# A reordered first stage and a spread first sweep in a fused attention, gated MLP and token/channel mixer kernel

## The chip, the core and the metric

One Trainium2 chip, one core. The metric is the device time of one execution in microseconds. Before the change it is 1242.53 us, the median of 3 runs (1241.91 to 1242.74). The execution that was profiled took 1244.85 us, of which the traced span is 1242.3 us.

## The reference, cut

Three layers follow each other, for 8 batches of 576 tokens (S) and 512 features:

```python
# 1: attention in chunks of 64 tokens, 8 heads of 64
scores = scale * q_c @ k_c.T; attn = exp(scores - max); attn /= sum + 1e-9
x = attn @ v_c                                   # (8, 576, 512)
# 2: gated MLP with a product over tokens
h = relu(x @ w_in); u, v = h[..., :512], h[..., 512:]
v_n = (v - mean(v)) / sqrt(var(v) + 1e-6)
x = (u * (w_spatial @ v_n + b_spatial)) @ w_out
# 3: mixer
u = x + (relu(x.T @ w_tok1) @ w_tok2).T
out = u + relu(u @ w_ch1) @ w_ch2                # d_tok 256, d_ch 1536
```

All inputs reach the kernel as 32-bit or 64-bit floats; `w_in`, `w_out` and the weights of the mixer come in 64 bits and are converted on the chip.

## The kernel before, in words

Each large product runs in a split form: an operand is kept as a rounded high part and a low part, and three matmuls (high by high, high by low, low by high: `PASSES`) take the place of one. So nearly every operand costs one cast on ACT (the high part) and one subtraction on DVE that waits for that cast (the low part).

The work has four parts. **The first stage** (about the first 120 us) does the attention and the gated MLP of batch 0, begins the attention of batch 1, and converts the weights on the way. **The steady stages** do the same for batches 1 to 6, with the attention of the next batch in between, and store each batch's result in device memory (`x2d`). **The last stage** does the gated MLP of batch 7 and in its gaps begins the mixer for batch 0. **The sweeps** do the mixer's channel half: eight sweeps of 21 groups for the first product (`ch1`), then eight of 7 for the second (`ch2`). The channel products use seven block products in place of eight, so they work on seven combinations of the operand (`comb_u`, 0 to 6) and of the weights (`Comb`, sets 0 to 3).

The order of the first, steady and last stages is written out by hand in three strings (`FIRST`, `STEADY`, `LAST`, from line 24). `play` (line 1169) reads them word by word; each word is one step, and each engine executes its instructions in the order in which they were so recorded. The words of the first stage that matter here, where a number behind the word is a unit, a column block or a piece:

- `x`, `S`, `s`, `e`, `n`, `z`, `T`, `t`, `P`, `p`, `q` are one head pair's attention: transposing q and k on DVE (line 377), scores on PE (391), the maximum and the subtraction on DVE (410, 411), exp on ACT (417), the sum on DVE (421), scaling on POOL (427), transposing on PE (435), its copy on ACT (443), the product with v on PE (459), and the result's high part on ACT (478) and low part on DVE (480). With an `a` ahead they belong to batch 0, without it to batch 1 here.
- `wl`, `wa`, `wm`, `we`, `wi`, `wk` (or `wj`) convert piece 0 to 11 of `w_in` and `w_out`: load (130), two scalings on ACT (144, 145), two bit operations on DVE (153, 155), an addition on POOL (163), the high part on ACT (185) and the low part on POOL or DVE (188). Pieces 0 to 3 are the rows of the half of `w_in` that makes v; pieces 4 to 7 are the columns of the half that makes u, one for each of `U0` to `U3`; pieces 8 to 11 are `w_out`.
- `gl`, `gt`, `gh` load `w_spatial`, transpose one column block on PE (246) and split it (83, 84; the last block 256, 257 and 262 to 264).
- `Y`, `V`, `R`, `r`, `F`, `G`, `rs`, `rq`, `N`, `i`, `Q` make v and normalize it: products on PE (536, 565), relu on ACT (583), statistics on DVE (588, 589), the fold of the last 64 tokens (574, 575, 579), the root (593 to 598), the normalization on DVE (602), and its split (608, 617). `U`, `E` make u (625, relu 635). `W`, `M`, `H`, `J` make the product over tokens and the gate (648, 658, 661, 664), `A`, `B`, `O`, `D` the output product (674, 681).

Two PSUM buffers tie steps together. `turn_ws` (the word `gt`) and `pv` (the word `P`) write the same buffer, tag `p`, of which there is one; so a `P` waits until the `gh` ahead of it has read the transposed block, and the reverse. `U` and `W` rotate through two buffers, so `U2` waits for the relu of `U0`.

In the mixer, the token half of batch b+1 runs inside sweep b, one step after each group (`tok_steps`, line 936): `b_nat` (860) transposes 128 token rows on DVE (866), rounds them on ACT (868) and makes the low part on DVE (870 or 873) in one go; `b_tok1` (879) multiplies them on PE (887, 891, 893); `b_tok2` (919) makes the second token product (926), which DVE adds (931). Ahead of sweep 1 the steps for batch 1 have already begun at the end of `LAST` (`st`, `st2`), and all seven `comb_u` of batch 0 are made there (`cu0` to `cu6`; casts 967, low parts 968, differences 974). In sweep 1 the weights of the groups 7 to 20 are still to be made: the dictionary `fill` lists which step of `comb_steps` (casts 821, low parts 825, sums on POOL 809 to 813) follows which group. `ch1_out` (1033) reads the results (1039 to 1051, 1030).

Of the kernel before, what the change touches and what calls it, by code (L numbers as in the profile page):

```python
# [23 lines left out]
FIRST = """  # L24
al0 wl0 al1 wl1 Z9 ax0 ay0 wa0 aS0 as0 ax1 al2 av0 wl2 wm0 ae0 ay1 an0 we0 az0 aS1 as1 wa1 aT0 wi0 wm1
at0 ax2 al3 av1 wl3 we1 wk0 ae1 ay2 an1 az1 aP0 aS2 ap0 as2 wi1 aq0 aT1 wa2 ae2 at1 ax3 av2 wm2 ay3 an2
az2 aP1 av3 aS3 as3 ap1 ae3 aq1 wj1 ax4 ay4 aT2 we2 wa3 wi2 at2 an3 wm3 az3 gl0 gl1 gl2 wl4 wl5 aP2 aS4
as4 ap2 wk2 we3 aq2 Y0 ae4 aT3 at3 wi3 an4 wk3 az4 Y1 aP3 L0 ap3 aq3 wa4 aT4 at4 Y2 aP4 wm4 ap4 aq4 Y3
x0 we4 wl6 wa5 L1 gt0 wi4 R0 R1 gh0 wm5 r0 S0 V2 s0 wk4 R3 we5 gt1 wi5 F r1 e0 R2 r3 wa6 G r2 gh1 wk5
U0 wl7 n0 x1 R4 z0 wm6 gt2 r4 we6 rs rq gh2 wi6 S1 U1 E0 wk6 s1 N0 T0 gt3 wa7 i0 Q0 t0 e1 gh3 N1 U2  # L30
wm7 n1 N2 we7 gt4 i1 wi7 E1 z1 Q1 gh4 wk7 i2 N3 N4 L2 wl8 U3 i4 Q2 x2 P0 p0 L3 S2 i3 E2 Q3 T1 q0 Q4
W0 t1 E3 s2 wl9 wa8 wm8 wa9 W1 we8 x3 e2 M0 M1 wi8
wm9 S3 W2 n2 wl10 we9 H0 wa10 W3 M2 s3 H2 wi9 J0 wl11 M3 z2 P1 S4 wk8 H1 J1 wj9 p1 q1 J2 H3
e3 wm10 T2 J3 A0 s4 n3 we10 A1 wa11 t2 L4 z3 wi10 B0 wm11 D0 e4 B1 P2 p2 D1 we11 T3 wj10 O2 n4
q2 t3 x4 z4 L5 P3 T4 wi11 p3 q3 D2 wk11 t4 O3 P4 D3 p4 q4
"""
# [19 lines left out]
def attention_gmlp_mixer(  # L56
# [794 lines left out]
    def b_load(b, m):  # L851
# [7 lines left out]
                in_=x2d[b][:, 32 * e:32 * e + 32].rearrange("(t j) i -> j t i", j=32))  # L859
        raws[b, m] = raw  # L860

    def b_nat(b, m):
# [5 lines left out]
        nc.scalar.copy(out=xn[:, 0], in_=nat)  # L868
        if m < 4:
            nc.vector.tensor_tensor(  # L870
                out=xn[:, 1], in0=nat, in1=f32(xn[:, 0]), op=ALU.subtract)
        else:
            nc.vector.tensor_tensor(
                out=xn[64:128, 0], in0=nat[64:128], in1=f32(xn[64:128, 0]), op=ALU.subtract)
# [4 lines left out]
    def b_tok1(b, m, xn):
        if m == 0:  # L880
            tok[b] = [PB["ps_t"].tile([128, 512], F32, tag="t", name="ps_h1") for _ in range(2)]
        ps = tok[b]
        for kk in range(2):
            ksl = slice(128 * kk, 128 * kk + 128)
            if m < 4:
                for n, (p, r) in enumerate(PASSES):
                    nc.tensor.matmul(  # L887
                        ps[kk], lhsT=PB["w1"][r][:, m, ksl], rhs=xn[:, p],
                        start=m == 0 and n == 0, stop=False)
            else:  # L890
                nc.tensor.matmul(
                    ps[kk], lhsT=PB["w1r"][0][:, ksl], rhs=xn[:, 0], start=False, stop=False)
# [387 lines left out]
    put_in(0, 6, c1[2][1].load)  # L1280
    put_in(0, 7, s1[2][0][0])
    put_in(0, 8, *s1[2][0][1:3], s1[2][1][0])
    put_in(0, 9, s1[2][0][3], s1[2][1][1])
    put_in(0, 10, s1[2][0][4], s1[2][1][2])
    put_in(0, 11, s1[2][1][3])
    put_in(0, 12, s1[2][1][4])
# [105 lines left out]
```

## Time and profile before

| | |
|---|---|
| median of 3 runs | 1242.53 us |
| the profiled execution: own time, span | 1244.85 us, 1242.3 us |
| PE busy (matmuls) | 1192.9 us, 96% of the span |
| DVE, ACT, POOL busy | 879.5 us (71%), 501.0 us (40%), 161.7 us (13%) |
| mean granted TensorE clock | 0.984 |
| DMA | 196.00 MB, mean 158 GB/s |

The rows of the profile give a start in us from the span's start, a duration in us, the engine, the line, the operation, the tiles written and read and their shapes; in square brackets stands the idle time of that engine just before, and what ended it. "PE" rows are matmuls; a run of equal ones is one row. In the tables by stretch each engine has its busy time and the number of its instructions, and then come the granted clock, the DMA share and the rate. The profiled execution's own time is 2.55 us longer than its span (1244.85 - 1242.3): this lies around the traced instructions.

### The profile page before, as it was taken

How to read it: one execution, taken by the hardware profiler on the slowest of the kernel's cores; microseconds unless marked ns; L12 is line 12 of the kernel's file. 1: busy time of each engine (PE TensorE's matmuls, PEld its weight loads, DVE VectorE, ACT ScalarE, POOL GpSimd, SP SyncE). 2: the span in 40 equal slices, each digit the busy share in tenths (PEclk: the TensorE clock that was granted, in tenths of full speed). 3: DMA queues.
4: the chain of work that ended last, by engine and by line, in shares of the span. 5: the costliest groups of instructions: out<-in, count | busy, mean ns of one | idle time of the engine just before them, and what ended most of it. 6: DMA issues, size and time to landing. Idle time of an engine off the chain costs nothing. (4 is left out here: it accounts for less than half of the span.)

```text
span 1242.3 us, 25079 instructions
## 1 busy us (share of the span) xinstructions
PE 1192.9 (96%) x10042; PEld 1127.6 (91%) x10042; DVE 879.5 (71%) x1365; ACT 501.0 (40%) x797; POOL 161.7 (13%) x156
## 2 busy tenths in 40 slices
...
GB/s 228 150 77 127 96 104 134 100 172 107 200 85 206 89 213 38 56 158 203 140 142 170 170 189 172 163 187 166 134 303 190 195 217 199 183 188 189 214 213 45
DMA packets 405704, 196.00 MB, mean 158 GB/s; under 512 B 348434, under 2 KB 368338, under 8 KB 405588
## 3 DMA queue, kind: packets, MB, share of 16 engines
...
q8 instruction: 79, 1.29, 0.5%
...
HBM read 123.16 MB, written 71.17 MB: 156 GB/s over the span
## 5 line engine op out<-in xcount | busy, mean ns | idle before, releaser
L1010 PE MATMUL ps_c<-ub,wt 128*128 128x288 f32 x2016 | 288.9, 298 | 6.6 <-ACT s L1042 2.5
L1010 PEld LDWEIGHTS ps_c<-ub,wt 128*128 128x128 f32 x2016 | 278.2, 190 | 12.9 <-ACT s L1042 3.8
L1010 PE MATMUL ps_c<-hb,wt 128*128 128x288 f32 x2016 | 268.9, 295 | 1.6 <-DVE hb L1099 1.6
L1010 PEld LDWEIGHTS ps_c<-hb,wt 128*128 128x128 f32 x2016 | 268.2, 188 | 2.2 <-DVE hb L1099 2.2
L625 PE MATMUL ps_u<-xt,w_in 128*128 128x288 f32 x768 | 110.3, 304 | 7.7 <-ACT ut L635 3.3
L625 PEld LDWEIGHTS ps_u<-xt,w_in 128*128 128x128 f32 x768 | 107.3, 195 | 9.1 <-ACT ut L635 3.5
L1098 ACT CAST hb<-h 128x1728 fp32r<-128x1728 f32 x40 | 64.8, 1638 | 122.7 <-DVE h L1091 50.0
L648 PE MATMUL ps_s<-ws,vn 128*128 128x288 f32 x768 | 108.5, 297 | 2.8 <-ACT ut L635 2.8
L648 PEld LDWEIGHTS ps_s<-ws,vn 128*128 128x128 f32 x768 | 103.5, 188 | 4.7 <-ACT ut L635 4.4
L674 PE MATMUL ps_o<-g,w_out 128*128 128x288 f32 x768 | 106.6, 296 | 0.0
L674 PEld LDWEIGHTS ps_o<-g,w_out 128*128 128x128 f32 x768 | 102.5, 188 | 1.0 <-ACT h L899 0.2
L1099 DVE TENSOR_TENSOR hb<-h,hb 128x1728 fp32r<-128x1728 f32 x40 | 78.2, 1955 | 28.6 <-ACT hb L1098 28.6
L536 PE MATMUL ps_v<-w_in,xt 128*128 128x512 f32 x384 | 92.7, 399 | 0.0
L536 PEld LDWEIGHTS ps_v<-w_in,xt 128*128 128x128 f32 x384 | 72.1, 190 | 16.7
L427 POOL TENSOR_TENSOR e<-e,sm 128x512 f32<-128x512 f32 (+1 forms) x40 | 39.1, 976 | 236.6 <-DVE sm L423 194.3
L163 POOL TENSOR_TENSOR ctmp<-ctmp,craw 128x512 uint32<-128x512 uint32 (+3 forms) x41 | 49.6, 1211 | 135.4 <-DVE ctmp L155 64.6
L926 PE MATMUL ps_u<-w,h 128*128 128x288 f32 x384 | 62.2, 299 | 4.4 <-DVE xh L931 4.4
L967 ACT CAST ub<-xh 128x576 fp32r<-128x576 f32 x56 | 37.4, 672 | 70.0 <-DVE xh L974 66.8
L926 PEld LDWEIGHTS ps_u<-w,h 128*128 128x128 f32 x384 | 54.8, 190 | 5.7 <-DVE xh L931 5.5
L968 DVE TENSOR_TENSOR ub<-xh,ub 128x576 fp32r<-128x576 f32 x56 | 43.0, 770 | 21.1 <-ACT ub L967 20.6
L868 ACT CAST xn<-nat 128x512 fp32r<-128x512 f32 x40 | 24.8, 619 | 76.8 <-DVE nat L866 75.6
L887 PE MATMUL ps_h<-xn,w 128*128 128x512 f32 x192 | 51.8, 403 | 3.4 <-ACT xn L868 3.3
...
## 6 DMA issues: line engine op xcount, KB each, us to landing
hd<-c SPq DMA_DIRECT2D x120, 288.0 KB, 2.2
...
```

The costliest lines, as they stand in the source:

```text
L163: nc.gpsimd.tensor_tensor(out=tu, in0=tu, in1=raw[:, :, 0], op=ALU.add)
L427: nc.gpsimd.tensor_tensor(out=e, in0=e, in1=sm.to_broadcast([128, e.shape[1], 64]), op=ALU.mult)
L536: nc.tensor.matmul(ps, lhsT=self.xt[kc][:, p, 128 * ti:128 * ti + 128], rhs=w_in_t[r][:, kc, DM:2 * DM], start=kc == 0 and n == 0, stop=kc ...
L625: nc.tensor.matmul(ps[:, h, 0:HALF], lhsT=w_in_t[r][:, kc, 128 * m:128 * m + 128], rhs=self.xt[kc][:, p, HALF * h:HALF * h + HALF], start= ...
L648: nc.tensor.matmul(ps[:, h, 0:HALF], lhsT=lhsT, rhs=rhs[:, HALF * h:HALF * h + HALF], start=n == 0, stop=n == len(ops) - 1)
L674: nc.tensor.matmul(ps[:, h, 0:HALF], lhsT=w_out_t[r][:, kc, 128 * m:128 * m + 128], rhs=self.g[p][:, kc, h], start=kc == 0 and n == 0, sto ...
L887: nc.tensor.matmul(ps[kk], lhsT=PB["w1"][r][:, m, ksl], rhs=xn[:, p], start=m == 0 and n == 0, stop=False)
L926: nc.tensor.matmul(ps, lhsT=h1[:, kk, p, 128 * m:128 * m + 128], rhs=PB["w2"][r][:, kk, HALF * h:HALF * h + HALF], start=n == 0, stop=n == 5)
L968: eng.tensor_tensor(out=lo, in0=x, in1=f32(hi), op=ALU.subtract)
L1010: nc.tensor.matmul(ps, lhsT=lhsT, rhs=rhs, start=first and n == 0, stop=n == len(ops) - 1, skip_group_check=True)
L1098: nc.scalar.copy(out=hi, in_=x)
L1099: nc.vector.tensor_tensor(out=lo, in0=x, in1=f32(hi), op=ALU.subtract)
```

## The change

Four things change; no instruction's size does, and the number of matmuls stays.

- **`FIRST` is written in another order.** The copy `at2` stands ahead of the copies `ay4`. The transposes of `w_spatial` begin ahead of `Y0`. Pieces 6 and 7 are loaded at once after pieces 4 and 5, into the buffer that pieces 0 and 1 used (`load_piece`, tag `g0`), ahead of the q, k and v of batch 1; their conversion `wa6`, `wa7` comes after the root `rq`, and `P0` stands ahead of `U2`.
- **`LAST` makes only `cu0` to `cu3`.** `cu4`, `cu5` and `cu6` follow groups 0, 1 and 2 of sweep 1. The first cast of the second weights (`pr1`) stands behind the first `st2` and `cu1`.
- **`fill` is spread.** Of the second weights, the later casts and low parts of both halves come one group later each.
- **`b_nat` leaves its low part owed.** `pay` records it at the next `b_nat`, at the next `b_tok1` or behind the next group's matmuls, so that DVE has other rows between the transpose and the subtraction.

```diff
@@ FIRST (all lines differ; one of them)
-U0 wl7 n0 x1 R4 z0 wm6 gt2 r4 we6 rs rq gh2 wi6 S1 U1 E0 wk6 s1 N0 T0 gt3 wa7 i0 Q0 t0 e1 gh3 N1 U2
+i2 gh4 wk6 P0 n1 wm7 L2 wl8 U2 Q2 N3 i3 z1 we7 p0 E2 N4 i4 wi7 Q3 q0 x2 wk7 T1 t1 U3 S2 Q4 s2 E3 W0 P1
@@ LAST
-y3 B0 D0 m0 m1 cl3 y4 y5 B1 D1 m2 st st m3 y6 O2 D2 m4 m5 y7 pr0 m6 m7 O3 left cu0 end
-pr1 st2 cu1 st2 cu2 pr2 cu3 st2 cu4 cu5 cu6
+y3 B0 D0 m0 m1 cl3 y4 y5 B1 D1 m2 st m3 y6 O2 D2 m4 st m5 y7 pr0 m6 m7 O3 left cu0 end
+st2 cu1 pr1 st2 cu2 pr2 st2 cu3
@@ b_nat, b_tok1 and the loop of the sweeps
+    owed = []
+    def pay():
+        while owed:
+            owed.pop()()
     def b_nat(b, m):
+        pay()
...
         nc.scalar.copy(out=xn[:, 0], in_=nat)
-        if m < 4:
-            nc.vector.tensor_tensor(
-                out=xn[:, 1], in0=nat, in1=f32(xn[:, 0]), op=ALU.subtract)
...
+        r, p = (slice(0, 128), 1) if m < 4 else (slice(64, 128), 0)
+        owed.append(lambda: nc.vector.tensor_tensor(
+            out=xn[r, p], in0=nat[r], in1=f32(xn[r, 0]), op=ALU.subtract))
     def b_tok1(b, m, xn):
+        pay()
...
             ch1(b, g, i)
+            pay()
             ch1_out(b, g, i)
@@ load_piece
-        if i < 4:
+        if i < 4 or 6 <= i < 8:
...
-                    [128, 2, DM, 2], U32, tag=f"g{i // 2}", bufs=1, name="wv_raw")
+                    [128, 2, DM, 2], U32, tag=f"g{i // 2 % 3}", bufs=1, name="wv_raw")
@@ fill of sweep 1 (the steps of the weights for groups 7 to 13; those for 14 to 20 likewise)
-    put_in(0, 0, *s1[1][0][1:3])
-    put_in(0, 1, s1[1][1][0], s1[1][0][3])
-    put_in(0, 2, s1[1][0][4], *s1[1][1][1:3])
-    put_in(0, 3, s1[1][1][3])
-    put_in(0, 4, s1[1][1][4])
-    put_in(0, 5, c1[2][0].load)
...
+    for n, fs in enumerate(((k0[1], k0[2]), (k1[0],), (k1[1], k1[2], k0[3]), (k0[4],), (k1[3],),
+                            (k1[4], c1[2][0].load), (c1[2][1].load,))):
+        put_in(0, n, *([lambda n=n: comb_u(0, n + 4)] if n < 3 else []), *fs)
```

How the instructions move shows at two places. The lines of the changed kernel are shifted: by one less up to the mixer, by some lines more behind `b_nat`.

The first place is in the first stage. On PE, around the last transpose of `w_spatial` (the rows with 64 partitions; `w_in_84` and `w_in_85` are the high and the low part of `w_in`), there stood before:

```order
L625 MATMUL ps_u<-xt,w_in_84 128x288 x2
L246 MATMUL ps_w<-ident,ws_rows 64x128 x4
L246 MATMUL ps_w<-ident,ws_rows 64x64
L625 MATMUL ps_u<-xt,w_in_84 128x288 x2
L625 MATMUL ps_u<-xt,w_in_85 128x288 x2
```

and now:

```order
L624 MATMUL ps_u<-xt,w_in_84 128x288 x2
L245 MATMUL ps_w<-ident,ws_rows 64x128 x4
L245 MATMUL ps_w<-ident,ws_rows 64x64
L458 MATMUL ps_p<-aT,vt 64x64 x16
L624 MATMUL ps_u<-xt,w_in_84 128x288 x2
L624 MATMUL ps_u<-xt,w_in_85 128x288 x2
```

The transpose was followed by `U3`; now it stands a block earlier, ahead of `U2`, and `P0`, which needs the same PSUM buffer, stands between them. On ACT, at the same place, there stood before (`vn_92` and `vr_94` are high parts of the normalized v, `ws_r_90` and `ws_r_91` the last block of `w_spatial`):

```order
L635 ACTIVATE ut<-ps_u 128x576
L144 ACTIVATE ctmp<-craw 128x512
L145 ACTIVATE craw<-craw 128x512
L608 CAST vn_92<-v_162 128x512
L443 COPY aT<-ps_t 128x512
L417 ACT_TABLE_LOAD
L417 ACTIVATE e<-e 128x512
L83 CAST ws_88<-ps_w 128x576
L608 CAST vn_92<-v_163 128x512
L185 CAST w_in_84<-ctmp 128x4x128
L635 ACTIVATE ut<-ps_u 128x576
L256 CAST ws_r_90<-ps_w 64x576 x2
```

and now:

```order
L143 ACTIVATE ctmp<-wv_raw 128x512
L144 ACTIVATE wv_raw<-wv_raw 128x512
L607 CAST vn_92<-v_164 128x512
L255 CAST ws_r_90<-ps_w 64x576 x2
L261 CAST ws_r_91<-ws_rows 1x576
L262 CAST ws_r_91<-ws_rows 1x576
L607 CAST vn_92<-v_165 128x512
L477 CAST xt<-ps_p 128x512
L634 ACTIVATE ut<-ps_u 128x576
L607 CAST vr_94<-v_166 128x512
L609 CAST vr_95<-v_166 64x512
L184 CAST w_in_84<-ctmp 128x4x128
```

Before, piece 7's scalings and its high part stood ahead of the casts of `w_spatial`'s last block; now the scalings stand just ahead of them and the high part nine rows behind them, after the relu of `U2`.

The second place is on DVE between the last stage and sweep 1 (`nat` and `xn` are token rows of batch 1, `ub` the low parts of the operand's combinations, `xh` its differences or, with 288 columns, the token product's additions). There stood before:

```order
L931 TENSOR_TENSOR xh<-ps_u,xh 128x288 x5
L968 TENSOR_TENSOR ub<-xh,ub 128x576
L974 TENSOR_TENSOR xh<-xh 128x576
L866 STREAM_TRANSPOSE nat<-x_raw 128x512
L870 TENSOR_TENSOR xn<-nat,xn 128x512
L968 TENSOR_TENSOR ub<-xh,ub 128x576
L974 TENSOR_TENSOR xh<-xh 128x576
L866 STREAM_TRANSPOSE nat<-x_raw 128x512
L870 TENSOR_TENSOR xn<-nat,xn 128x512
L968 TENSOR_TENSOR ub<-xh,ub 128x576 x2
L866 STREAM_TRANSPOSE nat<-x_raw 128x512
L873 TENSOR_TENSOR xn<-nat,xn 64x512
```

and now:

```order
L935 TENSOR_TENSOR xh<-ps_u,xh 128x288 x3
L972 TENSOR_TENSOR ub<-xh,ub 128x576
L978 TENSOR_TENSOR xh<-xh 128x576
L876 TENSOR_TENSOR xn<-nat,xn 128x512
L872 STREAM_TRANSPOSE nat<-x_raw 128x512
L972 TENSOR_TENSOR ub<-xh,ub 128x576
L978 TENSOR_TENSOR xh<-xh 128x576
L876 TENSOR_TENSOR xn<-nat,xn 128x512
L872 STREAM_TRANSPOSE nat<-x_raw 128x512
L972 TENSOR_TENSOR ub<-xh,ub 128x576
L876 TENSOR_TENSOR xn<-nat,xn 128x512
L872 STREAM_TRANSPOSE nat<-x_raw 128x512
```

Each low part `xn` stood right behind its transpose `nat`; now a low part `ub` stands between them, and with it, for the first two, a difference `xh`.

More of the change, by code (lines that the diff above doesn't have):

```diff
@@ L26 @@
 at0 ax2 al3 av1 wl3 we1 wk0 ae1 ay2 an1 az1 aP0 aS2 ap0 as2 wi1 aq0 aT1 wa2 ae2 at1 ax3 av2 wm2 ay3 an2
-az2 aP1 av3 aS3 as3 ap1 ae3 aq1 wj1 ax4 ay4 aT2 we2 wa3 wi2 at2 an3 wm3 az3 gl0 gl1 gl2 wl4 wl5 aP2 aS4
-as4 ap2 wk2 we3 aq2 Y0 ae4 aT3 at3 wi3 an4 wk3 az4 Y1 aP3 L0 ap3 aq3 wa4 aT4 at4 Y2 aP4 wm4 ap4 aq4 Y3
-x0 we4 wl6 wa5 L1 gt0 wi4 R0 R1 gh0 wm5 r0 S0 V2 s0 wk4 R3 we5 gt1 wi5 F r1 e0 R2 r3 wa6 G r2 gh1 wk5
-U0 wl7 n0 x1 R4 z0 wm6 gt2 r4 we6 rs rq gh2 wi6 S1 U1 E0 wk6 s1 N0 T0 gt3 wa7 i0 Q0 t0 e1 gh3 N1 U2
[L31 to L35, printed above, removed]
+az2 aP1 av3 aS3 as3 ap1 aq1 wj1 ae3 aT2 at2 ax4 ay4 we2 an3 wa3 wi2 az3 wm3 gl0 gl1 gl2 wl4 wl5 wl6 wl7
+aP2 aS4 as4 ap2 aq2 wk2 ae4 aT3 at3 we3 an4 wi3 gt0 wk3 az4 Y0 gh0 wa4 L0 aP3 ap3 aq3 wm4 Y1 gt1 we4 wa5
+aT4 at4 gh1 wm5 wi4 Y2 x0 aP4 ap4 aq4 we5 wk4 L1 Y3 gt2 R0 R1 R3 R2 r0 wi5 S0 gh2 r1 V2 F r2 r3 s0 wk5
+G R4 e0 U0 r4 rs rq x1 n0 z0 wa6 gt3 N0 gh3 i0 E0 wm6 S1 T0 t0 U1 Q0 N1 we6 i1 s1 gt4 e1 wi6 E1 Q1 N2 wa7
+i2 gh4 wk6 P0 n1 wm7 L2 wl8 U2 Q2 N3 i3 z1 we7 p0 E2 N4 i4 wi7 Q3 q0 x2 wk7 T1 t1 U3 S2 Q4 s2 E3 W0 P1
+e2 p1 q1 L3 wl9 n2 wa8 wm8 z2 W1 we8 x3 M0 wi8 wa9 wm9 T2 t2 S3 W2 s3 M1 H0 wl10 we9 e3 n3 J0 z3 P2 p2
+W3 M2 H1 wi9 wa10 q2 J1 wk8 S4 wl11 H2 M3 wm10 T3 t3 s4 J2 H3 e4 we10 wj9 J3 A0 P3 p3 n4 wa11 A1 wi10 q3
+L4 z4 B0 wm11 D0 B1 D1 T4 t4 we11 wj10 O2 P4 p4 wi11 q4 D2 wk11 x4 L5 O3 D3
 """
@@ L868, in b_nat @@
         nc.scalar.copy(out=xn[:, 0], in_=nat)
-        if m < 4:
-            nc.vector.tensor_tensor(
-                out=xn[:, 1], in0=nat, in1=f32(xn[:, 0]), op=ALU.subtract)
-        else:
-            nc.vector.tensor_tensor(
-                out=xn[64:128, 0], in0=nat[64:128], in1=f32(xn[64:128, 0]), op=ALU.subtract)
+        r, p = (slice(0, 128), 1) if m < 4 else (slice(64, 128), 0)
+        owed.append(lambda: nc.vector.tensor_tensor(
+            out=xn[r, p], in0=nat[r], in1=f32(xn[r, 0]), op=ALU.subtract))
         return xn
```

12 lines of the change are left out of this document (5 added, 7 removed).

## The prediction

> **What bounds the kernel now.** I read the page first, then the busy time of each engine by stretches cut at the stages, then PE's timeline in the two stretches that the change touches, and last the other engines there.
>
> ```profile
> PE 1192.9 (96%) x10042; PEld 1127.6 (91%) x10042; DVE 879.5 (71%) x1365; ACT 501.0 (40%) x797; POOL 161.7 (13%) x156
> ```
>
> The stretches have the columns start:end, length, then busy time and count of PE, PE's weight loads, DVE, ACT and POOL, then granted clock, DMA share and rate:
>
> ```profile
> 0.00:85.20 85.20, 63.61 (x669) 54.11 (x669) 52.08 (x103) 45.88 (x85) 27.61 (x28) 0.86 0.73 152
> 85.20:566.00 480.80, 478.31 (x4763) 444.64 (x4764) 320.99 (x647) 227.21 (x422) 89.39 (x81) 1.00 0.56 126
> 566.00:650.00 84.00, 73.17 (x428) 64.85 (x427) 60.89 (x92) 30.95 (x56) 19.91 (x24) 0.92 0.55 162
> 650.00:1242.30 592.30, 577.82 (x4187) 564.01 (x4185) 445.56 (x524) 196.99 (x237) 24.83 (x24) 1.00 0.62 183
> ```
>
> PE is the bound. It is idle for 1242.3 - 1192.9 = 49.4 us, and two stretches hold 32.4 of them: 85.20 - 63.61 = 21.6 up to the first product over tokens (`W0`), and 84.00 - 73.17 = 10.8 around sweep 1. In the same two the clock falls, to 0.86 and 0.92. The steady stages leave 2.5 us in 481, and behind 650 the change moves no more than the one low part that is now owed. So what is won or lost ahead of `W0` and in 566 to 650 should reach the end whole. The change touches just these two, and can win no more than their idle and half-clock time.
>
> **The first stage.** PE's timeline, before. A row is a run of equal matmuls; in brackets the idle time before it, and who ended it:
>
> ```profile
> 31.65 1.06 PE L459 MATMUL ps_p<-aT,vt 64*64 64x64 f32 x32 [3.56 <-ACT aT L443]
> 33.46 3.85 PE L536 MATMUL ps_v<-w_in,xt 128*128 128x512 f32 x12
> 37.50 3.02 PE L536 MATMUL ps_v<-w_in,xt 128*128 128x512 f32 x12
> 55.25 4.98 PE L625 MATMUL ps_u<-xt,w_in 128*128 128x288 f32 x24 [3.18 <-ACT v L583]
> 66.34 3.45 PE L625 MATMUL ps_u<-xt,w_in 128*128 128x288 f32 x24
> 70.78 0.80 PE L246 MATMUL ps_w<-ident,ws_rows 128*64 128x128 f32 x5 [0.99 <-DVE ws L84]
> 74.91 0.85 PE L625 MATMUL ps_u<-xt,w_in 128*128 128x288 f32 x2 [3.33 <-ACT ut L635]
> 76.95 5.65 PE L625 MATMUL ps_u<-xt,w_in 128*128 128x288 f32 x22 [1.20 <-POOL w_in L188]
> 85.20 3.46 PE L648 MATMUL ps_s<-ws,vn 128*128 128x288 f32 x24 [0.27 <-ACT ut L635]
> ```
>
> A `U` takes 3.45 us; `U0` (4.98) and `U3` (0.85 + 5.65 = 6.50) ran at a lowered clock, which cost 1.53 and 3.05 us. The clock shows it:
>
> ```profile
> 54.00:60.00 6.00, 4.75 (x24) 4.75 (x25) 5.06 (x13) 4.62 (x8) 1.25 (x2) 0.72 1.01 157
> 72.00:84.00 12.00, 7.90 (x83) 7.27 (x85) 8.28 (x15) 5.93 (x11) 4.09 (x3) 0.57 0.01 1
> ```
>
> Both slow spells stand behind waits of over 3 us. Now the new order, step by step.
>
> *Up to `U0`: won.* `at2` no longer stands behind the copies and the conversions that held it; I put 2.1 of the 3.56 us as gone. Then the transpose `gt0` stands in between, and waits until the high and low parts `aq2` have read the shared PSUM buffer. So `Y0` begins at about 34.7, 1.2 later than 33.46, but at full clock (3.02 for 3.85), and `gt0`, `gt1` (0.80 each) are then behind us. `Y3` ends near 48.5. The relus `R0` to `R3` follow at once, so the wait of 3.18 goes; with `gt2` (0.8), `S0` (1.1) and `V2` (2.0) `U0` begins at about 52.1 and ends at 55.4 at full clock. Before it ended at 60.1: 4.7 us ahead here.
>
> *`S1`: a new wait.* The transposes `x1` stand on DVE behind `G`, `R4`, `r4` and `rs`, and these behind `s0` and four statistics. The pieces:
>
> ```profile
> 54.49 0.67 DVE L579 TENSOR_TENSOR v<-ps_v,v_sum 128x512 f32<-128x512 f32 x1
> 56.73 0.63 ACT L583 ACTIVATE v<-v 128x512 f32<-128x512 f32 x1
> 55.23 0.69 DVE L588 BATCH_NORM_STATS2 st<-v 128x6 f32<-128x512 f32 x1
> 62.09 0.61 DVE L593 TENSOR_SCALAR rs<-mv 128x5 f32<-128x5 f32 x1
> 58.64 0.71 DVE L377 STREAM_TRANSPOSE qkT<-qk_raw 128x512 f32<-128x512 f32 x1
> 60.12 0.38 DVE L153 TENSOR_SCALAR ctmp<-ctmp 128x512 uint32<-128x512 uint32 x1
> ```
>
> The transposes take 60.12 - 58.64 = 1.48. With nothing queued ahead the chain from `V2` (52.1), over two copies of about 0.6, gives 52.1 + 1.2 + 0.67 + 0.63 + 0.87 + 0.8 + 1.48 = 57.8; with `s0` and `e0` ahead of the copies it is near 60. I take 59.2. PE is through with `gt3` at 56.1, so it waits 3.1 us (1.7 to 4). `T0` then waits, by my estimate, about 1.1 for POOL's `z0`, and `U1` runs from 62.0 to 65.4. That is where `U1` stood before (61.87), but `T0` and `gt3` are already done.
>
> *`P0`: a wait moved ahead of `U2`.* `gt4` ends at 66.1. `P0` writes the same PSUM buffer, so it waits for `gh4`. On ACT ahead of it stand `E1`, the two scalings of `wa7` and `i2`:
>
> ```profile
> 64.11 0.65 ACT L635 ACTIVATE ut<-ps_u 128x576 f32<-128x576 f32 x1
> 64.65 0.67 ACT L144 ACTIVATE ctmp<-craw 128x512 f32<-128x512 f32 x1
> 73.68 0.62 ACT L185 CAST w_in<-ctmp 128x512 fp32r<-128x512 f32 x1 [1.86 <-POOL ctmp L163]
> 74.75 1.26 ACT L256 CAST ws_r<-ps_w 64x576 fp32r<-64x576 f32 x2
> 76.04 0.67 ACT L262 CAST ws_r<-ws_rows 1x576 fp32r<-1x576 f32 x1
> 75.19 1.71 POOL L188 TENSOR_TENSOR w_in<-ctmp,w_in 128x512 fp32r<-128x512 f32 x1
> ```
>
> From `E1` at 65.5: 0.65 + 2 x 0.67 + 0.62 + 1.26 = 69.4, and DVE's low part (about 0.75) and its queue end it at 69.5 to 70.8. PE waits 3.4 to 4.7 us there. Before, no `U` waited for `gh4`; that is the price of the swap in the first order shown above.
>
> *`U3`: its weights come later.* `U2` runs from 71.6 and ends at 75.0 at full clock, at 76.7 if that wait lowers the clock as in 72:84. The high part `wi7`, which before stood ahead of the relu of its neighbour, now stands behind the relu `E2` and two casts `vr` (second order shown): 75.9 + 0.65 + 2 x 0.6 + 0.62, then POOL's 1.71, gives 79.9 to 80.6. So `U3` starts some 3 us after `U2` ends. `W0` comes at 84.4 with `U3` and `S2` at full clock, at 87.3 at half clock. I take 86.0 for 85.20: **+0.8** (-0.8 to +2.1, and to +5 with every queue at its worst). The 4.7 us won by `U0` are thus given back at `S1`, `P0` and `U3`.
>
> *After `W0`.* `S3` waits for `x3`, and the third pass of `A0` for the low part `J2`, which stand closer to their users now. No row shows either; the nearest is the short wait of 0.99 for a low part at 70.78. I take **+1.0** for both (0 to 2).
>
> *Loads.* Pieces 6 and 7 (1 MB) move ahead of q and k of batch 1. In 54 to 60 the DMA engines were full, so `x0` comes later; it stands ahead of `Y3`, and `S0`, which needs it, behind `Y3` and `gt2`. So nothing, with 1 us as the end of the range.
>
> **The first sweep.** PE's timeline, before:
>
> ```profile
> 577.90 1.92 PE L887 MATMUL ps_h<-xn,w 128*128 128x512 f32 x6 [1.55 <-ACT xn L868]
> 590.43 1.86 PE L1010 MATMUL ps_c<-ub,wt 128*128 128x288 f32 x12 [1.29 <-ACT s L1042]
> 598.24 1.07 PE L926 MATMUL ps_u<-w,h 128*128 128x288 f32 x6 [0.95 <-DVE xh L931]
> 605.38 1.81 PE L926 MATMUL ps_u<-w,h 128*128 128x288 f32 x6 [2.10 <-DVE xh L931]
> 606.99 2.50 PE L1010 MATMUL ps_c<-ub,wt 128*128 128x288 f32 x12
> 609.33 0.96 PE L926 MATMUL ps_u<-w,h 128*128 128x288 f32 x6
> 610.13 1.75 PE L1010 MATMUL ps_c<-ub,wt 128*128 128x288 f32 x12
> 621.62 2.80 PE L887 MATMUL ps_h<-xn,w 128*128 128x512 f32 x6 [1.78 <-ACT xn L868]
> 624.22 4.11 PE L1010 MATMUL ps_c<-ub,wt 128*128 128x288 f32 x24
> 642.17 0.50 PE L891 MATMUL ps_h<-xn,w1r 128*128 128x512 f32 x1 [1.70 <-DVE xn L873]
> 644.64 5.66 PE L1010 MATMUL ps_c<-ub,wt 128*128 128x288 f32 x24
> ```
>
> Slow spells follow the waits of 2.10, 1.78 and 1.70 us. The first cost (1.81 - 0.96) + (2.50 - 1.75) = 1.60. The waits at 590 to 605 end when DVE, or ACT for it, has read a result: DVE was behind with the weights' low parts. With those a group later, and the operands' last three spread, waits of 1.29 + 0.95 + 2.10 and the spell of 1.60 should go: **-5.9**. On the other side, ahead of the sweep `ub` and a difference now stand between a transpose and its low part (the third order shown):
>
> ```profile
> L968 DVE TENSOR_TENSOR ub<-xh,ub 128x576 fp32r<-128x576 f32 x13 | 10.5, 818 | 5.1 <-ACT ub L967 5.1
> ```
>
> At 0.82 us each one such row ahead makes the wait of 1.55 at 577.90 about 2.3: **+0.7**. The waits at 621 and 642 are those of one chain (transpose, cast, low part), which the owed subtraction shortens for DVE but not for PE; DVE, with `comb_u` 4 to 6 added to the sweep, is then the later one. I leave them as they are. Sum of the sweep: -5.2. The ends: -2 if only the 2.10 us and part of a slow spell go; -8.5 if the wait at 621 goes too (1.78, and 2.80 - 1.92 and 4.11 - 2 x 1.75 for its slow spell, 3.3 in all).
>
> On the clock the Trainium skill, page "TensorE: Matmul & The Clock Gate", section "Part 1: The HAM clock gate (the "warmup" mystery)", says that the rate halves after an idle window of about 3.4 us. The trace differs: the rows above are slow behind 2.10 and 1.70 us of idleness. By that rule the spell of 1.60 would not hang on the wait of 2.10 and could stay, and the whole sum would be 1.6 us less of a gain; the same rule speaks against the change at `P0`, whose new wait reaches 3.4.
>
> **The sum.** 0.8 + 1.0 - 5.2 = -3.4 us. The profiled execution would go from 1244.85 to 1241.4. It stands 2.3 us above the median 1242.53, about the 2.55 us outside its span, so I carry the difference over: 1242.5 - 3.4 = 1239.1, **1239**. A measurement of this kernel can tell about 0.2%, 2.5 us.
>
> **The rivals.**
> *More gain (0.12).* `P0` and `U3` wait at the short ends, so the spell of 3.05 in 72:84 goes and `W0` stands near 83, and in the sweep the spell at 621 goes too: -2 + 1 - 8.5 = -9.5, 1233. For it: both stretches hold that much. Against: the wait for `wk7` rests on a fixed chain of five rows.
> *No change (0.25).* The sweep gives back 3 of its 5.9 us, because DVE is only late elsewhere (one group later for the weights, one operand more to make), or the slow spell stays: -2.5 + 2 = about 0, 1240 to 1245. For it: DVE's queue, not a single row, was late in 590 to 610.
> *Slower (0.19).* The waits ahead of `S1`, `P0` and `U3` (3.1, 4.7, 3) come so close that PE stays at half clock from `S1` to `W0`: `U1`, `U2` and `U3` each pay 1.5 to 3 and `W0` stands at 88.5 or later, +3.3; with +2 behind it and -2 in the sweep: +3.3, 1246. It decides from `W0` at 88 on. For it: the row 72:84, with 0.57 over 12 us behind one wait of 3.33. Against: `U1` should have a full spell of work behind `S1`.
> *The change doesn't do what it says.* "Sooner" holds for the loads of pieces 6 and 7 alone; by the order their conversion `wi7` comes later. This lies in all the cases above.
>
> **How the numbers follow.** Forecast 0.44 (1236.5 to 1240), more gain 0.12, no change 0.25, slower 0.19. Faster: 0.44 + 0.12 = 0.56; same 0.25; slower 0.19. The range of 8 in 10 leaves out the outer half of the gain case and most of the slower one: 1232.5 to 1245.5. The forecast's own range is 1236.5 to 1240.
>
> **What would show it.** `U0` at about 52 with no wait; a wait of about 3 us ahead of `S1` that DVE's L376 ends; one ahead of `P0` (L458) that the low part L256 or the cast L255 ends; `U3` behind POOL's L187; `W0` at 84 to 87. In the sweep: no wait over 1 us between the first step of `b_tok2` (L926) and the last, a longer one than 1.55 ahead of the second token group, and waits left at the end. `W0` beyond 88, or as much idle time in the sweep as the 10.8 us before, would make the prediction wrong, and so would a gain above 8 us.

## The result and the profile after

| | before | after |
|---|---|---|
| median (4 runs each) | 1242.63 us | 1258.66 us (1258.43 to 1261.93) |
| ratio, 95% interval | | 1.0128 (1.0114 to 1.0143) |
| profiled execution: own time, span | 1244.85, 1242.3 us | 1258.43, 1256.4 us |

The change makes the kernel 1.3% slower: 16 us by the medians, 14.1 us between the two profiled spans. The forecast was 3.4 us faster.

PE after, from the page, and below it PE's stretches after, cut at the places where the work is the same as before: `W0`, the first product `Y0` of batch 1, the first channel product, the last token rows of sweep 2, the end.

```profile
PE 1198.1 (95%) x10042; PEld 1131.8 (90%) x10042; DVE 884.2 (70%) x1365; ACT 501.3 (40%) x797; POOL 162.4 (13%) x156
```

```profile
0.00:91.41 91.41, 66.84 (x668) 56.90 (x669) 55.53 (x105) 46.91 (x86) 27.98 (x28) 0.83 0.66 151
91.41:132.64 41.23, 37.27 (x415) 35.04 (x411) 25.66 (x50) 16.76 (x33) 10.99 (x9) 0.96 0.39 86
132.64:593.47 460.83, 455.29 (x4422) 421.16 (x4419) 303.18 (x607) 215.09 (x397) 84.60 (x79) 1.00 0.56 129
593.47:702.66 109.19, 98.96 (x640) 91.29 (x638) 79.33 (x119) 36.86 (x64) 13.97 (x16) 0.95 0.55 160
702.66:1256.40 553.74, 539.76 (x3908) 527.46 (x3908) 420.49 (x485) 185.65 (x218) 24.82 (x24) 0.99 0.62 184
```

The same stretches before; the first of them is the 0.00:85.20 shown in the prediction:

```profile
85.20:119.45 34.25, 34.25 (x410) 32.94 (x410) 25.20 (x48) 17.54 (x35) 11.10 (x9) 1.00 0.54 118
119.45:579.65 460.20, 455.34 (x4422) 421.29 (x4419) 303.50 (x612) 215.02 (x396) 84.86 (x79) 1.00 0.57 130
579.65:689.34 109.69, 101.24 (x640) 93.30 (x638) 77.65 (x120) 35.97 (x63) 13.35 (x16) 0.94 0.54 156
689.34:1242.30 552.96, 538.48 (x3908) 525.97 (x3908) 421.10 (x486) 186.61 (x220) 24.83 (x24) 1.00 0.62 184
```

Read the second column, the length: +6.2, +7.0, +0.6, -0.5 and +0.8 us, 14.1 in all. So 13.2 us are lost by the end of the first stage, half of them behind `W0`, where before PE had no idle time at all. The sweeps, where 5.2 us were to be won, are even.

PE's timeline after, in the first stage (first the product `Y0` of batch 0, which took 3.85 before):

```profile
35.54 4.59 PE L535 MATMUL ps_v<-w_in,xt 128*128 128x512 f32 x12
...
54.52 3.35 PE L624 MATMUL ps_u<-xt,w_in 128*128 128x288 f32 x24
61.79 1.15 PE L390 MATMUL ps_s<-qkT,qkT 64*64 64x64 f32 x32 [3.28 <-DVE last L377]
64.91 5.54 PE L624 MATMUL ps_u<-xt,w_in 128*128 128x288 f32 x24
74.81 1.13 PE L458 MATMUL ps_p<-aT,vt 64*64 64x64 f32 x32 [3.74 <-DVE ws_r L256]
75.87 5.23 PE L624 MATMUL ps_u<-xt,w_in 128*128 128x288 f32 x24
84.35 0.53 PE L624 MATMUL ps_u<-xt,w_in 128*128 128x288 f32 x2 [2.82 <-ACT w_in L184]
85.70 4.71 PE L624 MATMUL ps_u<-xt,w_in 128*128 128x288 f32 x22 [0.82 <-POOL w_in L187]
91.41 3.45 PE L647 MATMUL ps_s<-ws,vn 128*128 128x288 f32 x24
101.68 1.15 PE L390 MATMUL ps_s<-qkT,qkT 64*64 64x64 f32 x32 [1.30 <-DVE qkT L376]
115.27 0.53 PE L673 MATMUL ps_o<-g,w_out 128*128 128x288 f32 x2 [0.65 <-DMA vt<-in_v_dram]
125.57 0.53 PE L673 MATMUL ps_o<-g,w_out 128*128 128x288 f32 x2 [1.19 <-ACT w_out L184]
126.93 4.71 PE L673 MATMUL ps_o<-g,w_out 128*128 128x288 f32 x22 [0.82 <-POOL w_out L187]
```

The wait of 3.18 ahead of `U0` is gone, as forecast, and the three new ones stand where they were forecast: `S1` 3.28, `P0` 3.74, `U3` 2.82 + 0.82. `Y0` was to run at full clock and took 4.59; `U1`, `U2` and `U3` run slowly too (5.54, 5.23, 0.53 + 4.71). Behind `W0` there are four waits and one more stretch at a lowered clock. (The wait of 0.65 is put down to a DMA here; in experiments 5 to 8 the same one ends with `J2`, DVE's low part of g.) From `U0` to `W0` it takes 36.9 us, before it took 85.20 - 55.25 = 29.95. This difference between two places is the better measure, since `W0` itself lies at 82.08 to 85.20 in the five profiled executions with the old first stage (the kernel before and experiments 2, 3, 4 and 11), while from `U0` to `W0` they take 28.5 to 29.95.

How did piece 7 get late? ACT, DVE and POOL after, in order of time: piece 7's second scaling, the low part `gh4` that DVE was waiting to make, piece 7's bit operation, its addition, its high part and its low part.

```profile
71.65 0.64 ACT L144 ACTIVATE wv_raw<-wv_raw 128x512 uint32<-128x512 uint32 x1
```

```profile
74.00 0.75 DVE L256 TENSOR_TENSOR ws_r<-ps_w,ws_r 64x576 fp32r<-64x576 f32 x1 [4.41 <-ACT ws_r L255]
...
77.20 0.38 DVE L152 TENSOR_SCALAR ctmp<-ctmp 128x512 uint32<-128x512 uint32 x1
```

```profile
79.16 1.63 POOL L162 TENSOR_TENSOR ctmp<-ctmp,wv_raw 128x512 uint32<-128x512 uint32 x1 [0.68 <-issue]
84.37 1.27 POOL L187 TENSOR_TENSOR w_in<-ctmp,w_in 128x512 fp32r<-128x512 f32 x1 [3.59 <-ACT w_in L184]
```

```profile
83.68 0.62 ACT L184 CAST w_in<-ctmp 128x512 fp32r<-128x512 f32 x1
```

The scalings were done at 72.3. DVE stood idle for 4.41 us with `gh4` at the head of its queue, and the bit operation, which had its input, stood behind it until 77.20. The addition ended at 80.8, and the high part stood on ACT behind a cast of v that waited for DVE until 81.11, behind `E2` and behind the casts of the last tokens, until 83.68. From 72.3 to 85.6, 13.3 us passed over operations of 0.4 to 1.6 us.

PE in the sweeps after:

```profile
614.21 1.06 PE L930 MATMUL ps_u<-w,h 128*128 128x288 f32 x6 [1.91 <-DVE xh L935]
654.24 0.77 PE L895 MATMUL ps_h<-xn,w1r 128*128 128x512 f32 x1 [2.87 <-DVE xn L876]
702.66 0.47 PE L895 MATMUL ps_h<-xn,w1r 128*128 128x512 f32 x1 [1.71 <-DVE xn L876]
704.35 4.97 PE L1014 MATMUL ps_c<-ub,wt 128*128 128x288 f32 x24
```

The wait of 2.10 before `b_tok2` is still there (1.91), the last wait of sweep 1 has grown from 1.70 to 2.87, and sweep 2 has a new one of 1.71 with matmuls at a lowered clock behind it.

### The profile page after: what moved, and what is told of

Its sections match the earlier page's. It is cut to its first block, busy times and chain, and to the rows that moved or that the text cites. A ratio compares the mean times of both kernels' runs of the same rounds, so it can differ in the third digit from the quotient of the medians.

```text
span 1256.4 us, 25093 instructions
## 1 busy us (share of the span) xinstructions
PE 1198.1 (95%) x10042; PEld 1131.8 (90%) x10042; DVE 884.2 (70%) x1365; ACT 501.3 (40%) x797; POOL 162.4 (13%) x156
## 3 DMA queue, kind: packets, MB, share of 16 engines
q8 instruction: 79, 1.29, 0.5%
## 5 line engine op out<-in xcount | busy, mean ns | idle before, releaser
L162 POOL TENSOR_TENSOR ctmp<-ctmp,craw 128x512 uint32<-128x512 uint32 (+3 forms) x39 | 46.8, 1200 | 113.5 <-DVE ctmp L154 70.7
```

The lines of the kernel that those rows point to most:

```text
L162: nc.gpsimd.tensor_tensor(out=tu, in0=tu, in1=raw[:, :, 0], op=ALU.add)
```

## The experiments

Theory A: the first stage is bound by the chains through ACT, DVE and POOL that convert the weights and normalize v. The new order put waiting rows at the head of these queues, and PE only shows where it meets their results. The rivals are named where they are tested. Every ratio is against the kernel before, run at the same time as the experiment.

**1. The first stage alone.** The kernel before with only these edits:

```diff
-FIRST = """ (before)
+FIRST = """ (after)
-        if i < 4:
+        if i < 4 or 6 <= i < 8:
...
```

> The kernel before with only the first stage's new order and the shared load buffer of pieces 6 and 7; last stage, sweeps and fill as before. Theory A (the loss is made in the first stage, by conversions that stand later than their users): +13 us, about 1255.8, W0 near 91.4 and the first product of batch 1 near 132.6, sweep 1 with the same waits as before (10.8 us idle). Rival B (the first stage costs no more than the 6 us by which W0 is late, and the rest comes from the sweep): +6, about 1249.

Measured: 1255.09 us, ratio 1.0094 (1.0079 to 1.0109). `W0` at 91.36, `Y0` of batch 1 at 132.60. Theory A holds, B falls: the first stage makes 12 us by itself. (The profiled run, 1258.05 us, is the slowest of the four.)

**2. All but the first stage.** The changed kernel with these edits:

```diff
-FIRST = """ (after)
+FIRST = """ (before)
-        if i < 4 or 6 <= i < 8:
+        if i < 4:
...
```

> The changed kernel with the first stage's order and load buffers of before; last stage, owed low parts and the spread fill as changed. Theory A: the sweep wins 1.6 us up to its last token step and loses 3 us in a new wait of sweep 2, so +1 to +3, about 1244.5. Rival B: +8 to +10, about 1251. What the prediction said of the sweep: -5.2, about 1237.4.

Measured: 1244.25 us, ratio 1.0007 (0.9998 to 1.0017). That is at the low end of theory A's +1 to +3, and not told apart from the kernel before; the gain of the prediction is not there.

**3. The same, with nothing owed.**

```diff
             out=xn[r, p], in0=nat[r], in1=f32(xn[r, 0]), op=ALU.subtract))
+        pay()
         return xn
```

> As the kernel of the sweep's changes alone, but each low part of the token rows is made at once behind its transpose (the debt is paid inside b_nat). Theory A (the owed low part goes behind a low part of the operand that waits longer for ACT, and comes 1.3 us later to PE): the new wait of sweep 2 goes and the last wait of sweep 1 shrinks from 2.9 to about 1.7: -3 to -5 against the sweep's changes alone, about 1240. Rival C (the owed low part is harmless, and DVE is late by the added operands 4 to 6): the same time as the sweep's changes alone, within 1 us.

Measured: 1245.29 us, ratio 1.0022 (1.0014 to 1.0031). The new wait of sweep 2 is gone, as A said, and the last one of sweep 1 is 1.70 again. But A's gain of 3 to 5 us is a miss: by the time alone rival C (the same time) is as good, and only the trace speaks against it, since a larger wait has come ahead of the sweep. PE, DVE and ACT of this kernel there:

```profile
574.36 1.81 PE L932 MATMUL ps_u<-w,h 128*128 128x288 f32 x6 [4.94 <-DVE xh L937]
```

```profile
572.43 1.51 DVE L877 TENSOR_TENSOR xn<-nat,xn 128x512 fp32r<-128x512 f32 x1 [3.52 <-ACT xn L875]
573.86 0.81 DVE L937 TENSOR_TENSOR xh<-ps_u,xh 128x288 f32<-128x288 f32 x2
```

```profile
570.21 1.14 ACT L821 CAST wt<-c 128x512 fp32r<-128x512 f32 x2 [5.40 <-POOL c L813]
...
571.79 0.62 ACT L875 CAST xn<-nat 128x512 fp32r<-128x512 f32 x1
```

In the new `LAST` the second `st` stands five words later, behind `m4`. Its cast of token rows so stands on ACT behind two casts of weights that wait 5.40 us for POOL. A low part made at once waits 3.52 us for that cast, and the additions (L937) stand behind it. So this `LAST` is no better without the debt; and the debt costs elsewhere:

**4. Only the debt.** The kernel before with `owed` and `pay` alone.

```diff
+    owed = []
+    def pay():
+        while owed:
+            owed.pop()()
     def b_nat(b, m):
+        pay()
...
+        owed.append(lambda: nc.vector.tensor_tensor(
+            out=xn[r, p], in0=nat[r], in1=f32(xn[r, 0]), op=ALU.subtract))
     def b_tok1(b, m, xn):
+        pay()
...
             ch1(b, g, i)
+            pay()
             ch1_out(b, g, i)
```

> The kernel before with only the owed low part of the token rows; all orders and the fill as before. Theory A: one longer wait at the end of sweep 1 (1.70 becomes about 2.9) and a new wait of 1.7 with a slow spell of 1.5 in sweep 2: +3 to +5, about 1246.5. Rival C: within 1 us of before.

Measured: 1248.88 us, the runs from 1244.43 to 1250.76, ratio 1.0043 (1.0027 to 1.0059). Theory A's direction holds, C falls; the cost is about 5 us by the ratio, a little above A's +3 to +5. The profiled execution is the fastest of the six. In it PE waits 2.87 us at the end of sweep 1, 1.42 in sweep 2 (at full clock behind it, where A expected a slow spell), and this in the first groups of sweep 1, where before it waited 0.62:

```profile
589.21 0.47 PE L896 MATMUL ps_h<-xn,w1r 128*128 128x512 f32 x1 [3.56 <-DVE xn L877]
```

The waits add up to less than they seem to: those of 1.29, 0.95 and 2.10 that follow there in the kernel before are not in this execution. From `W0` to the end it takes 1160.3 us for 1157.1 before. Of these 3.2 us, 2.3 lie ahead of the first channel product and 1.3 in sweep 1. The wait of sweep 2 does not show in its length (47.12 us from the last token rows of sweep 1 to those of sweep 2, 47.17 before). The five other runs have a lower mean granted clock, 0.980 to 0.983 for 0.985; an estimate from that, 0.002 to 0.005 of 1242 us, is 2 to 6 us, about the spread. Where their clock fell no trace shows.

What makes a low part late stands on DVE. First the rows of the kernel before in sweep 2, then those of the changed one:

```profile
687.13 0.70 DVE L866 STREAM_TRANSPOSE nat<-x_raw 128x512 f32<-128x512 f32 x1
688.60 0.69 DVE L873 TENSOR_TENSOR xn<-nat,xn 64x512 fp32r<-64x512 f32 x1 [0.76 <-ACT xn L868]
```

```profile
698.71 0.70 DVE L872 STREAM_TRANSPOSE nat<-x_raw 128x512 f32<-128x512 f32 x1
701.03 0.76 DVE L972 TENSOR_TENSOR ub<-xh,ub 128x576 fp32r<-128x576 f32 x1 [1.62 <-ACT ub L971]
701.82 0.69 DVE L876 TENSOR_TENSOR xn<-nat,xn 64x512 fp32r<-64x512 f32 x1
```

Made at once, the low part waits 0.76 us for one cast and starts 1.47 us behind its transpose. Owed, it lets `ub` go ahead, which waits for the next cast on ACT (1.62), and starts 3.11 us behind. The debt was to fill a wait; here it exchanged a short one for a longer one.

**5. `P0` behind `U2` again.** The base of 5 to 8 is experiment 1; 9 stands on 6, and 10 on 9.

```diff
-i2 gh4 wk6 P0 n1 wm7 L2 wl8 U2 Q2
+i2 gh4 wk6 n1 wm7 L2 wl8 U2 P0 Q2
```

> Base is the kernel with only the new first stage (1255.1). P0 stands behind U2 again, all else stays. Theory A (waits in the order itself): the 3.74 us ahead of P0 go, but U3 still waits for piece 7, which DVE makes late; so W0 comes 2 to 3 us sooner than 91.4, the time is about 1252.5. Rival D (the waits cost little by themselves, the half clock does it): the clock stays down behind the wait at S1, W0 no more than 1 us sooner, about 1254.5.

Measured: 1256.92 us, ratio 1.0116 (1.0099 to 1.0133), no faster than its base. From `U0` to `W0` 37.3 us, as in the changed kernel. The wait of 3.74 went, one of 3.03 for POOL's `z1` came ahead of `T1`, and `U3` waited 5.14 instead of 2.82. The expected 2 to 3 us were a miss of theory A's numbers, and rival D's 1254.5 was nearer: `U3` starts when piece 7 is there, whatever PE did ahead of it.

**6. Piece 7 sooner.**

```diff
-E1 Q1 N2 wa7 i2 gh4 wk6 P0 n1 wm7 L2 wl8 U2 Q2 N3 i3 z1 we7 p0 E2 N4 i4 wi7 Q3 q0 x2 wk7 T1
+E1 Q1 N2 wa7 wm7 i2 gh4 wk6 we7 P0 n1 L2 wl8 U2 wi7 wk7 Q2 N3 i3 z1 p0 E2 N4 i4 Q3 q0 x2 T1
```

> Same base. P0 stays ahead of U2; piece 7's bit operations on DVE go ahead of the low part gh4, its addition ahead of z1 on POOL, its high part ahead of the relu E2. Theory A: the waits of 2.82 and 0.82 ahead of and in U3 go, W0 at about 87.5, the time about 1251. Rival D: U3 is reached sooner but runs at half clock as before, W0 at 88.5 to 89, about 1252.5.

Measured: 1248.96 us, ratio 1.0051 (1.0032 to 1.0071). PE:

```profile
74.22 1.13 PE L458 MATMUL ps_p<-aT,vt 64*64 64x64 f32 x32 [3.76 <-DVE ws_r L256]
75.28 5.21 PE L624 MATMUL ps_u<-xt,w_in 128*128 128x288 f32 x24
...
80.68 3.44 PE L624 MATMUL ps_u<-xt,w_in 128*128 128x288 f32 x24
```

`P0` still waits 3.76 and `U2` is still slow, yet `U3` follows at once and at full clock, and `U0` to `W0` takes 31.2 us. Four words moved on ACT, DVE and POOL bring back 6 us, more than theory A or rival D expected. That is 5.7 of the 6.9 us lost between `U0` and `W0`, nearly all of it the two waits of `U3` (2.82 + 0.82) and its slow clock (0.53 + 4.71 for 3.44). The bit operation now starts at 71.25 and the high part at 74.79, for 77.20 and 83.68. The four words were moved together; how much each of the three queues held back alone, no run shows.

**7. Both moves.** `P0` behind `U2` in the line above.

> Same base with both moves. Theory A: both waits go and they add, W0 at 82.5 to 84.5, the time 1246 to 1248; what is left over the kernel before is the loss behind W0 (7 us). Rival D: W0 at 86 or later, 1250 or more.

Measured: 1250.41 us, ratio 1.0068 (1.005 to 1.0085), `U0` to `W0` 31.0 us. The gains do not add: theory A's 1246 to 1248 is a miss, and the time is rival D's. But PE waits 3.61 us for POOL's `z1` ahead of `T1` instead: the wait moved once more, and `U3` runs slowly behind it (4.96).

**8. PE kept busy.** 18 and 22 idle transposes ahead of `S1` and `P0`.

```diff
+    def busy(n):
+        ps = ps_at.tile([128, 512], F32, tag="t", bufs=1, name="ps_w")
+        for _ in range(n):
+            nc.tensor.transpose(ps[:, 0:128], ident, ident)
...
-rs rq x1 n0 z0 wa6 gt3 N0
+rs rq x1 n0 z0 wa6 gt3 K18 N0
-i2 gh4 wk6 P0 n1
+i2 gh4 wk6 K22 P0 n1
```

> Same base, with 18 idle transposes (of the identity, to a PSUM tile that nobody reads) ahead of S1 and 22 ahead of P0, so that PE works in both waits; no wait is changed. Theory A with the clock as a part of the price: U1 and U2 run at full clock (3.45 instead of 5.5 and 5.2), W0 about 2 us sooner (U2 starts no sooner, but ends 1.8 sooner, and U3 waits for piece 7 all the same), about 1253. Rival D (the clock is the main price): W0 4 to 5 us sooner, about 1250.

Measured: 1257.14 us, ratio 1.011 (1.0087 to 1.0134). PE:

```profile
64.73 3.43 PE L624 MATMUL ps_u<-xt,w_in 128*128 128x288 f32 x24
75.22 3.46 PE L624 MATMUL ps_u<-xt,w_in 128*128 128x288 f32 x24
84.12 0.85 PE L624 MATMUL ps_u<-xt,w_in 128*128 128x288 f32 x2 [5.00 <-ACT w_in L184]
...
91.83 3.46 PE L647 MATMUL ps_s<-ws,vn 128*128 128x288 f32 x24
```

`U1` and `U2` now run at full clock, 3.43 and 3.46 for 5.54 and 5.23, and `W0` comes no sooner (`U0` to `W0` 37.1 us). Rival D falls for these two: the slow clock of `U1` and `U2` cost nothing, because `U3` waited for piece 7 anyhow. The price of 2 us that theory A gave it was a miss too. `U3` itself stays slow here (its second part takes 5.36); the 1.8 us of that clock come back only with the wait, in experiment 6.

**9. The waits behind `W0`.** On top of experiment 6:

```diff
-L3 wl9 n2 wa8 wm8 z2 W1 we8 x3 M0
+L3 wl9 n2 x3 wa8 wm8 z2 W1 we8 M0
-H2 M3 wm10 T3 t3 s4 J2 H3
+H2 J2 M3 wm10 T3 t3 s4 H3
-wj10 O2 P4 p4 wi11 q4 D2 wk11 x4 L5 O3 D3
+wj10 O2 wi11 wk11 P4 p4 q4 D2 x4 L5 O3 D3
```

> Base is the kernel with the new first stage and piece 7 sooner (1249.0, W0 at 85.1 like before, 41.0 us from W0 to the first product of batch 1 where before took 34.3). Three moves behind W0: the transposes x3 ahead of piece 8's bit operations, the low part J2 ahead of M3, and piece 11's high and low part (wi11, wk11) ahead of P4 and p4. Theory A (the 7 us are these three waits, 1.30 + 0.65 + 1.19 + 0.82, and the slow spell of 1.65 behind the last): 41.0 becomes 35 to 36, the time 1243 to 1244, the same as the kernel before. Rival E (DVE and ACT have too much to do there in this order, and another row is late in place of each): 39 or more, 1247 or more.

Measured: 1244.56 us, ratio 1.002 (1.001 to 1.0031). From `W0` to the first product of batch 1 36.7 us, for 41.0 to 41.2 and 34.25 before. So these three moves were 4.4 of the 7 us, a little less than theory A had. Waits of 0.35, 0.71 and 0.21 for other rows of DVE are left, in rival E's manner but smaller.

**10. `S1` and `P0` served too.** On top of 9:

```diff
-G R4 e0 U0 r4 rs rq x1 n0 z0
+x1 G R4 e0 U0 n0 z0 r4 rs rq
-N2 wa7 wm7 i2 gh4 wk6 we7 P0 n1 L2 wl8 U2 wi7 wk7 Q2 N3 i3 z1 p0
+N2 n1 wa7 wm7 i2 gh4 wk6 z1 we7 L2 wl8 U2 P0 wi7 wk7 Q2 N3 i3 p0
```

> The kernel above with P0 behind U2, the transposes x1 ahead of G, n1 and z1 ahead of the last block of w_spatial, so that S1, P0 and T1 find their inputs. Theory A: the waits at S1 (3.28) and P0 (3.76) go as well, W0 at 80 to 82, the time 1239 to 1241, below the kernel before. Rival E: W0 at 84 or later because DVE's low parts of the normalized v now come last, 1243 or more.

Measured: 1244.36 us, ratio 1.0016 (1.0006 to 1.0027). Theory A's number is a miss. PE:

```profile
57.16 1.15 PE L390 MATMUL ps_s<-qkT,qkT 64*64 64x64 f32 x32 [0.56 <-DVE last L377]
61.33 1.11 PE L434 MATMUL ps_t<-ident,e 128*128 128x128 f32 x4 [3.02 <-POOL e L426]
...
70.46 0.54 PE L624 MATMUL ps_u<-xt,w_in 128*128 128x288 f32 x2 [3.37 <-ACT w_in L184]
```

`S1` waits 0.56 instead of 3.28, and then `T0` waits 3.02 for POOL and `U2` 3.37 for piece 6. `U0` to `W0` takes 30.45, for the 29.95 of before. With the three inputs made ready, PE waits for two others, and the stretch is no shorter than in the old order.

**11. The spread weights alone.** The kernel before with the new `fill`, and `cu4` to `cu6` in it.

```diff
-pr1 st2 cu1 st2 cu2 pr2 cu3 st2 cu4 cu5 cu6
+pr1 st2 cu1 st2 cu2 pr2 cu3 st2
-    put_in(0, 0, *s1[1][0][1:3])
...
+        put_in(0, n, *([lambda n=n: comb_u(0, n + 4)] if n < 3 else []), *fs)
```

> The kernel before with the operands 4 to 6 moved into sweep 1 and the weights' steps spread, nothing else (last stage otherwise as before, low parts of the token rows made at once). As the prediction had it: the waits of 1.29, 0.95 and 2.10 and the slow spell go, -4 to -6, about 1237.5. Theory A (DVE has as much to do as before, so the wait comes back at the next token rows): within 1.5 us of before, about 1242.5.

Measured: 1241.02 us (11 runs), ratio 0.9983 (0.9974 to 0.9992): 2 us faster than the kernel before, the only part tested alone that gains, and the one version here that beats both kernels. PE:

```profile
595.72 1.06 PE L926 MATMUL ps_u<-w,h 128*128 128x288 f32 x6 [0.61 <-DVE xh L931]
600.28 1.06 PE L926 MATMUL ps_u<-w,h 128*128 128x288 f32 x6 [1.92 <-DVE xh L931]
614.87 1.86 PE L1010 MATMUL ps_c<-ub,wt 128*128 128x288 f32 x12 [0.80 <-ACT c L1051]
619.53 2.80 PE L887 MATMUL ps_h<-xn,w 128*128 128x512 f32 x6 [2.80 <-ACT xn L868]
```

The wait of 1.29 at 590 is gone, and that of 0.95 is 0.61. But the 2.10 is still 1.92, one of 0.80 stands at 614, and the next token rows wait 2.80 instead of 1.78. This pair is not the new fill's: experiments 1, 6 and 7, which have the old one, have it too (0.70, 0.47 and 0.27 ahead of 2.91, 2.81 and 2.80). Experiment 1:

```profile
636.48 2.93 PE L886 MATMUL ps_h<-xn,w 128*128 128x512 f32 x6 [2.91 <-ACT xn L867]
```

So single waits of this sweep differ from one execution to the next, and its length is the better measure: from the first channel product to the last token rows of sweep 1 it takes 60.86 us here. The nine profiled executions with the old fill and without the debt (before, 1, 5 to 10 and 12) take 62.37 to 63.16, the other three with the new fill (the changed kernel, 2 and 3) 60.76 to 61.28. The spread fill wins 1 to 2.4 us there in each of them. The time lies between the two expectations, and what theory A said of the next token rows is not shown.

**12. The loads alone.** The kernel before with `wl6 wl7` behind `wl5`.

```diff
-wl4 wl5 aP2
+wl4 wl5 wl6 wl7 aP2
...
-        if i < 4:
+        if i < 4 or 6 <= i < 8:
...
```

> The kernel before with only the loads of pieces 6 and 7 moved ahead, into the buffer of pieces 0 and 1. Theory A (loads are not what any step of the first stage waits for): within 1 us of before. Rival F (1 MB ahead of the loads of q, k and v of batch 1 holds those up, so that part of the loss is the loads'): +2 to +4.

Measured: 1242.40 us, ratio 0.9998 (0.9988 to 1.0007). No difference; rival F falls. Loading the two pieces sooner by itself neither helps nor hurts.

## Why the prediction was wrong

*Right in what it read.* PE is the bound, and what is lost in the first stage reaches the end whole. The waits at `S1`, `P0` and `U3` come, at about the sizes given (3.28, 3.74 and 2.82 + 0.82 for 3.1, 3.4 to 4.7 and about 3). The slower rival, given 0.19, had the right place and picture: `U1` and `U2` run slowly and `W0` lies beyond 88. Its price, +3.3 in all, was far too small, and its cause, the lowered clock of `U1` and `U2`, has no price (experiment 8).

*Failed: "The change touches just these two".* Half of the loss lies from `W0` to the first product of batch 1, where PE had no idle time before, and the sweep is even.

*Failed: "`W0` comes at 84.4 ... 87.3 ... I take 86.0".* +0.8 was +6.2; `W0` came 5.4 us behind the forecast. Of these 2.4 are there at `U0`. `Y0` was to begin at 34.7 "at full clock (3.02 for 3.85)"; it began at 35.54 and took 4.59, and 4.50 to 4.64 in every profiled execution with the new order. So `U0` came at 54.52 for 52.1, and "4.7 us ahead" was 2.4 at its end (57.87, before 60.23). What these 2.4 us cost at `W0` no run shows. The other 3.0 lie between `U0` and `W0`. There the sum went through PE's waits, and put the lowered clock of `U2` into the price. Experiment 8 shows that the slow clock of `U1` and `U2` has no price, 5 and 7 that the wait at `P0` has none, and 6 that piece 7 has 5.7 of the 6.9 us lost there against before. The prediction had the chain of piece 7 in its `U3` step but began it at the end of `U2`. It missed the start: `wm7` had moved on DVE behind `gh4`, whose wait of 4.41 us for ACT held it. ACT in turn came to the relu `E1` at 70.55, where the prediction had 65.5; with `U1` at full clock (experiment 8) it still came at 70.34.

*Failed: "After `W0` ... I take +1.0".* It was +7.0. `x3` (1.30) and `J2` (0.65) were named and came to 1.95, inside the 0 to 2 given. Piece 11 was not: its high part stood on ACT behind `p4`, which waits for `P4`, and cost 1.19 + 0.82 and a lowered clock of 1.65 (4.71 for about 3.06, an estimate from the 3.34 that 24 such matmuls take before). The prediction followed the conversions up to `W0` and stopped there, though the diff moved `wi11` and `wk11` as well. Experiment 9 gets 4.4 of the 7 us back by three moves. About 1.4 us of the 7 lie in no single row, and stay open.

*Failed: "waits of 1.29 + 0.95 + 2.10 and the spell of 1.60 should go: -5.9".* The spread fill alone brings 2 us (experiment 11). The spell had no price to win back: the kernel before, which has it, takes 62.52 us from the first channel product to the last token rows of sweep 1, and experiment 12, which has the same wait without it, 62.37. And "DVE was behind with the weights' low parts" was only half the reason. Ahead of the wait of 2.10 DVE stood idle, before:

```profile
602.21 1.29 DVE L825 TENSOR_TENSOR wt<-c,wt 128x512 fp32r<-128x512 f32 x2 [1.73 <-ACT wt L821]
```

The cast that this low part waited for had itself waited 4.93 us on ACT for a sum on POOL (L813). In experiment 11 DVE works without a gap ahead of the 1.92 that is left. One group later, the rows are late for another reason.

*Failed: the owed low part, "shortens for DVE but not for PE".* Where a `ub` goes ahead it lengthens the way to PE: by 1.64 us at the place shown (3.11 - 1.47), and the last wait of sweep 1 by 1.17 (2.87 for 1.70). Alone it costs about 5 us (experiment 4). "Behind 650 the change moves no more than the one low part" was true, and it was not free: in the changed kernel sweep 1 is 1.75 us shorter (60.77 for 62.52), and from there to the last token rows of sweep 2 it takes 1.25 longer (48.42 for 47.17). Experiment 2, which has the debt and the new fill, is not told apart from before (interval 0.9998 to 1.0017).

By the ratios, experiments 1 and 2 add to 1.0101, with the whole change at 1.0128. The 3 us between are about as large as the intervals together; between the profiled spans (+13.2, +0.6, whole +14.1) there is nothing missing. Whether the two parts add up fully stays open. So does the spread of experiment 4, 6 us between its runs, of which one profile shows only the fastest.
